# A linear-attention and softplus-FFN kernel: z turned in 32x32 blocks on VectorE and written as rows, and the first two FFN blocks taken through the weights together

## The chip, the cores and the metric

The kernel runs on one core of a Trainium2 chip. Five engines work side by side, each through its own queue in order: TensorE (PE, with its weight loads PEld), VectorE (DVE), ScalarE (ACT), GpSimd (POOL) and SyncE (SP). SyncE only issues DMAs here, and all DMAs of the kernel are issued by it. An instruction waits at the head of its queue until what it needs is there, and all that is queued behind it waits too. The metric is the device time of one execution in microseconds, the median over several runs.

## The reference

Attention with random features for 8 batches of 8 heads, 576 tokens, 64 dimensions and 128 features, then a feed-forward network with softplus over all 4608 tokens:

```python
q_p, k_p = phi(q * scale), phi(k * scale)     # exp(x @ omega.T - |x|^2/2 - max) / sqrt(m)
kv = np.einsum('bhsm,bhsd->bhmd', k_p, v)
z = np.sum(k_p, axis=2)
num = np.einsum('bhsm,bhmd->bhsd', q_p, kv)
den = np.einsum('bhsm,bhm->bhs', q_p, z)[..., None] + 1e-06
x = (num / den)                               # (4608, 512) after a transposition of heads
h = x @ w_in                                  # 512 -> 2048
g = np.maximum(h, 0.0) + np.log1p(np.exp(-np.abs(h)))
out = g @ w_out                               # 2048 -> 512
```

## The kernel before

Heads are handled in quads of four: 16 quads, two for each batch. For a quad, keys and queries come in five units of tokens (u = 0 to 4). A unit is loaded (L369 to L377 for batches 0 and 1, L489 and L494 later), squared and summed for its norms, split into a rounded part and a rest (L508, L512), projected on TensorE (L400 or L518), joined, reduced to its maximum, and exponentiated on ScalarE (L437 or L542). Keys are multiplied with v (L606, or L662 in batch 0); the last such product of a quad gives kv and, in an extra column, z.

What is done with z matters here. z of a quad lies as 128 partitions (features) by 4 (heads), and den needs it as rows of 128 features spread over all partitions. In batch 0 TensorE does this (`rows`, L686). In the 14 later quads it goes through DRAM: `z` (L616, VectorE) writes the tile, `out_z` (L624) stores it across, so that each element of 4 bytes is a piece by itself, and `in_z` (L628) reads the 4 x 128 numbers back as one row, broadcast to 128 partitions, as zb. `den` (L729, VectorE) multiplies the query features with zb and sums; `invert`, `divide` (L738, VectorE or GpSimd) and `blocks` (L761) follow; the turned features go through DRAM once more (L771, L774 out, L784 in), and `num` (L852) makes x, which is kept as a rounded part xh and a rest xl.

The FFN takes x in blocks: four of 256 tokens and seven of 512. For each of 16 slices fc of the hidden layer, `plan_step` lays 12 matmuls into h (L902 to L904), softplus on ScalarE and VectorE (L908 to L925), and 3 matmuls for every 128 tokens into acc (L931 to L933). The 32 weight slices are loaded at the start (L283) as 64-bit words and converted on ScalarE and VectorE (L291 to L310); wi and wo of a slice are needed by the first block that uses it.

No order is written by hand. Every step is a `Work` with the engines that can run it, costs, a due time and the buffers that it takes; `in_order` lays all of them out greedily by assumed costs, and due times say who goes first among those that can start. The numbers in the tables (LATE, PATIENCE, the offsets on each `due`) set the order and nothing else. `with_fill` puts matmuls without use (`fill`, L1043) where it expects TensorE to wait. For out_z the planner of before assumes `dma(1.3, 1.6, 0.3)`: 1.3 us until the transfer starts, 1.6 on the wires, 0.3 until it has landed.

The eight banks of PSUM are two for "at", two for "h" and four for "acc". Projections of batch 1 draw on "at" and "acc" (`room["more"]`).

Of the kernel before, what the change touches and what calls it, by code (L numbers as in the profile page):

```python
# [19 lines left out]
P = 128  # L20
# [13 lines left out]
AHEAD = 213.44  # L34
MARGIN = 0.00

LATE = {"num": 1.25, "turn": 5.44, "project": 0.85, "blocks": 0.00, "out": 0.27, "in": 2.55, "store": 0.24, "outer": 0.27}
START = {"SP": 0.75, "ACT": 1.9, "PE": 4.6}
SLOW = 7.59
FILL = 5.58  # L40
UNTIL = 93.76
HEAT = 2.95
EXTRA = 0.00
WINDOW = 3.4133
PATIENCE = {"PE": 0.00, "DVE": 0.01, "ACT": 0.00, "POOL": 1.23, "SP": 1.02}
LEAN = {"DVE": 0.81, "POOL": 0.50, "ACT": 0.00}
SPREAD = ((0, 24.76), (18.30, 71.16))
# [136 lines left out]
def favor_softplus_kernel(ctx, tc, q0, k0, qx, qy, kx, ky, vv, om, wi, wo, out):  # L184
# [16 lines left out]
    at.tile([P, 80], F32, name="gap")  # L201
# [72 lines left out]
    def plan_weights(nm, fc, due):  # L274
# [34 lines left out]
        def low_part(e):  # L309
# [5 lines left out]
            "SP", dma(0.65, 1.22, 1.7), due - 2.62, load, spare={} if last else {"w": 2},  # L315
# [5 lines left out]
        a = do(("ACT", "DVE"), (aw, dw2), due - 3.09, low_bits, after=[l], port=True)  # L321
        b = do("ACT", aw, due + 0.16, rebias, after=[l])
        c = do("DVE", dw, due - 3.03, joined, after=[a, b], port=True)
        d = do(
            ("ACT", "DVE"), (aw, dw), due + 0.20, high_part, after=[c] + (in_w if last else []), take=[("w", box, "w")], port=True,
# [3 lines left out]
        return do(("DVE", "POOL"), (dw, pw), due - 6.73, low_part, after=[d], give=[(box, "raw")], port=True)  # L329
# [14 lines left out]
    def plan_unit(q, kind, us, due, early):  # L344
# [83 lines left out]
        def exponent(j):  # L428
# [12 lines left out]
            "SP", read(size), due - 9.14, load, behind=prev.get("load"),  # L441
# [3 lines left out]
        if kind == "k" and not early:  # L445
            for i in range(len(us)):
                ldv.append(do(
                    "SP", dma(0.7, 1.0, 0.7), due + 28.88, lambda i=i: load_v(i), behind=ld, take=[("v", b, ("vs", i))]
                ))
        s = do(("POOL", "ACT"), (pool(w), act(w)), due + 7.71, squares, after=[ld])  # L450
        r, sm = None, [("sm", b, "sms")]
        if not cols:
            r = do("DVE", dve(w), due + 2.54, norms, after=[s], behind=prev.get("norms"), take=sm)
# [3 lines left out]
            "PE", 0.19 + (0.46 if cols else 0.23) * nt, due - 2.23, project, after=[ld] + ([s] if cols else []),  # L457
# [19 lines left out]
        for i in range(len(us)):  # L477
            plan_queries(q, us[i], due - 5.54 * i, b, es, f"{nm}_{i}", i, i == len(us) - 1)

    def plan_split(q, kind, u, due):  # L480
# [59 lines left out]
        def exponent(t):  # L540
# [4 lines left out]
            "SP", read(n * (P + D) * P * 4), due - 46.21, load, behind=prev.get("load"), take=[("x", b, "x")],  # L545
        )
        prev["load"], ldv = ld, []
        if kind == "k":
            ldv = [do("SP", dma(0.7, 1.0, 0.7), due + 5.80, load_v, behind=ld, take=[("v", b, ("vs", 0))])]
        s = do(("POOL", "ACT"), (pool(n * D), act(n * D)), due + 8.16, squares, after=[ld])  # L550
        h = do(("ACT", "DVE"), (act(n * P), dve(n * P, 2)), due - 4.34, rounded, after=[ld], take=[("ts", b, "ts")], port=True)
        h = do(("DVE", "POOL"), (dve(n * P) + 0.12, 1.12 * pool(n * P)), due - 0.80, rest, after=[h, parted], give=[], port=True)
        r = do(
            "DVE", dve(n * D), due + 20.76, norms, after=[s, h], behind=prev.get("norms"), take=[("sm", b, "sms")],
# [4 lines left out]
            "PE", 0.118 * n, due - 1.78, project, after=[h], behind=(prev.get("project"), q.zc if kind == "q" else None),  # L559
# [5 lines left out]
        for t in range(n // 2):  # L565
            a = do(
                "ACT", act(2 * M, PSUM), due + 0.31, lambda t=t: aside(t), after=[p], behind=a,
                take=[] if t else [("ph", b, ("phs", 0))], spare={"ph": 1}, soon={} if t or n < 4 else {p: 0.22},
            )
            es.append(do("DVE", dve(2 * M), due - 1.57, lambda t=t: join(t), after=[a], give=[(b, ("ppb", t))]))  # L570
        m = do("DVE", dve(n * M), due + 6.81, maxima, after=es + [r])
        m = do("DVE", 0.33, due - 0.16, bias, after=[m], port=True)
# [20 lines left out]
    def plan_sums(q, keys, due, deps):  # L593
# [20 lines left out]
        def z():  # L614
            q.z = at.tile([P, 16], F32, name=f"z{q.nm}", tag=q.slots["z"], bufs=1)[:, :4]
            nc.vector.scalar_tensor_tensor(q.z, y["kv"][:, :, D], rm, q.kvp[:, :, D], ALU.mult, ALU.add)  # L616

# [4 lines left out]
        def out_z():  # L622
            q.zd = dram.tile([4, P], F32, name=f"zd{q.nm}", tag="zd", bufs=2)
            nc.sync.dma_start(q.zd.rearrange("c m -> m c"), q.z)  # L624
# [9 lines left out]
        for k, (b, i, u) in enumerate(keys):  # L634
            m = do(
                "PE", 0.836 if u < 4 else 0.418, due + 0.62, lambda k=k: outer(k), after=[m] if k else [x for x, _ in deps],
# [4 lines left out]
        if first:  # L641
            q.part = do("ACT", 0.29, due - 25.64, part, after=[m] + ([quads[q.n - 1].kvl] if q.n > 2 else []), give=[(y, "bank")])
            return
        a = do("DVE", 0.1, due - 8.97, z, after=[m, q.part], take=[("z", q.slots, "z")])
        q.kvl = do("DVE", 0.35, due + 7.75, whole, after=[m, a] + old, give=[(y, "bank")])
        r = do("SP", dma(1.3, 1.6, 0.3), due - 18.33, out_z, after=[a], give=[(q.slots, "z")])
        q.zc = do("SP", dma(1.7, 1.6, 0.95), due + 34.19, in_z, after=[r], take=[("zb", q.slots, "zb")])

    def plan_early_keys(q, u, due, b, es):

        def outer():
# [15 lines left out]
            "PE", 0.836 if u < 4 else 0.418, due + 27.40, outer, after=es + [q.kvm], heat=1040,  # L667
# [6 lines left out]
        def z():  # L674
            q.z = at.tile([P, 16], F32, name=f"z{q.nm}", tag=q.slots["z"], bufs=1)[:, :4]
# [15 lines left out]
        def copy():  # L691
# [3 lines left out]
        a = do("DVE", 0.07, due + 29.06, z, after=[q.kvm], take=[("z", q.slots, "z")])  # L695
        q.kvl = do("ACT", 0.32, due + 4.48, high, after=[q.kvm, a], give=[(q.slots, "kv")])
        r = do(
            "PE", 0.86, due + 12.41, rows, after=[a], heat=2048, take=[("any", q.slots, "zp"), ("zb", q.slots, "zb")],
            give=[(q.slots, "z")],
        )  # L700
        q.zc = do("ACT", 0.48, due - 14.62, copy, after=[r], give=[(q.slots, "zp")])
# [10 lines left out]
    def plan_queries(q, u, due, bu, es, nm, first, last):  # L712
# [65 lines left out]
        def in_blocks(qt, o, sizes):  # L778
# [13 lines left out]
            "DVE", 0.87, due - 2.57, den, after=es + [q.zc], steps=4, soon={es[1]: 0.43} if q.b > 1 and u < 4 else {},  # L792
# [3 lines left out]
        d = do("DVE", 0.09, due + 0.43, invert, after=[d])  # L796
# [356 lines left out]
```

## Time and profile before

| | us |
|---|---|
| median of 3 runs | 1118.53 |
| lowest, highest | 1115.6, 1123.72 |
| profiled execution, its own time | 1131.58 |
| its span | 1129.8 |
| granted TensorE clock, mean | 0.962 |

The profile is of one execution. Busy times say how long an engine worked; a wait in a timeline stands in brackets ahead of the instruction that ended it, with the instruction that released it behind the arrow. The granted clock is 1 or 0.5 at any moment; a mean of 0.95 over a stretch says that a tenth of it ran at half. A matmul's duration contains its way through the array, so consecutive matmuls overlap: the distance of their starts is what one costs. For a DMA the table of issues gives the time from issue to landing.

### The profile page before, as it was taken

The page shows a single profiled execution, that of the slowest core. Times are in us where ns is not written, and L with a number is a line of the kernel's source. Part 1 is how long each engine was busy: PE and PEld are TensorE (multiplying, and loading weights), DVE is VectorE, ACT ScalarE, POOL GpSimd, SP SyncE. Part 2 cuts the span into 40 slices and gives each one's busy share as a digit, 9 for nine tenths or more (in the row PEclk, how much of TensorE's full clock was granted, in tenths as well). Part 3 has the DMA queues.
Part 4 walks back from the last instruction along what each step waited for, and adds up shares of the span by engine and source line. Part 5 has one row for each costly group of instructions (what it writes and reads, how often), then busy time and mean ns, then how long its engine had stood idle before and what let it go on. Part 6 is the DMA issues. An engine that isn't in the chain of part 4 may idle for free. (4 is left out here: it accounts for less than half of the span.)

```text
span 1129.8 us, 17905 instructions
## 1 busy us (share of the span) xinstructions
PE 1044.1 (92%) x5609; PEld 867.4 (77%) x5609; DVE 752.5 (67%) x2345; ACT 762.1 (67%) x1946; POOL 147.9 (13%) x173
## 2 busy tenths in 40 slices
PE   9689898998998989898979998979899799999998
PEld 6578786887886878687768786868778687888886
DVE  5899675776877867787867786868667733222222
ACT  6999666776867766777677786757665645444443
POOL 0021212122221211212110111102010100000000
PEclk9899898999998989899989999989989899999999
DMA  9941554534544446545454645563245402000001
GB/s 338 349 155 52 62 160 113 148 104 103 161 103 148 113 131 106 149 135 138 94 135 135 136 113 106 159 129 96 83 124 99 107 15 80 1 1 19 19 1 38
DMA packets 123278, 125.82 MB, mean 111 GB/s; under 512 B 23216, under 2 KB 98096, under 8 KB 123184
## 3 DMA queue, kind: packets, MB, share of 16 engines
q1 hardware_dynamic: 123184, 124.68, 41.5%
q8 instruction: 45, 0.74, 0.3%
q14 instruction: 49, 0.40, 0.1%
HBM read 98.66 MB, written 25.98 MB: 110 GB/s over the span
## 5 line engine op out<-in xcount | busy, mean ns | idle before, releaser
L902 PE MATMUL h<-xh,wi 128*128 128x512 f32 (+1 forms) x704 | 255.6, 363 | 4.6 <-DVE u L917 4.6
L903 PE MATMUL h<-xl,wi 128*128 128x512 f32 (+1 forms) x704 | 251.1, 357 | 0.0
L904 PE MATMUL h<-xh,wi 128*128 128x512 f32 (+1 forms) x704 | 250.1, 355 | 0.0
L931 PE MATMUL acc<-wo,gh 128*128 128x512 f32 x576 | 233.7, 406 | 0.0
L932 PE MATMUL acc<-wo,gh 128*128 128x512 f32 x576 | 229.9, 399 | 0.0
L933 PE MATMUL acc<-wo,gl 128*128 128x512 f32 x576 | 229.2, 398 | 0.0
L917 DVE SCALAR_TENSOR_TENSOR u<-h,u 128x512 f32<-128x512 f32 (+1 forms) x176 | 103.1, 588 | 160.2 <-ACT u L914 159.1
L908 ACT ACTIVATE u<-h 128x512 f32<-128x512 f32 (+1 forms) x176 | 91.2, 519 | 134.9 <-PE h L904 130.4
L902 PEld LDWEIGHTS h<-xh,wi 128*128 128x128 f32 x704 | 136.8, 194 | 28.9 <-DVE u L917 5.7
L903 PEld LDWEIGHTS h<-xl,wi 128*128 128x128 f32 x704 | 136.5, 194 | 18.4
L904 PEld LDWEIGHTS h<-xh,wi 128*128 128x128 f32 x704 | 135.9, 193 | 18.8
L921 ACT CAST gh<-u 128x512 fp32r<-128x512 f32 (+1 forms) x172 | 93.2, 542 | 58.4 <-PE acc L933 27.6
L933 PEld LDWEIGHTS acc<-wo,gl 128*128 128x128 f32 x576 | 110.9, 193 | 24.6
L931 PEld LDWEIGHTS acc<-wo,gh 128*128 128x128 f32 x576 | 110.9, 193 | 24.0 <-issue 4.5
L932 PEld LDWEIGHTS acc<-wo,gh 128*128 128x128 f32 x576 | 111.1, 193 | 17.8
L925 DVE TENSOR_TENSOR gl<-u,gh 128x512 fp32r<-128x512 f32 (+1 forms) x120 | 77.6, 647 | 52.4 <-ACT gh L921 51.5
L911 ACT ACTIVATE u<-u 128x512 f32<-128x512 f32 (+1 forms) x176 | 97.4, 555 | 3.1
L914 ACT ACTIVATE u<-u 128x512 f32<-128x512 f32 (+1 forms) x176 | 97.1, 554 | 2.5
L729 DVE CUSTOM_DVE_ANT_0 restq<-phq,zb 128x128 f32<-128x128 f32 x280 | 73.5, 294 | 18.9 <-DMA zb<-zd 11.2
L542 ACT ACTIVATE phk<-phk,smk 128x128 f32<-128x128 f32 x216 | 70.1, 392 | 11.7 <-DVE smk L538 11.6
L925 POOL TENSOR_TENSOR gl<-u,gh 128x256 fp32r<-128x256 f32 (+1 forms) x56 | 50.3, 900 | 182.2 <-ACT gh L921 158.0
L738 POOL TENSOR_TENSOR phq<-phq,dnq 128x512 f32<-128x512 f32 (+1 forms) x44 | 40.7, 925 | 254.0 <-DVE dnq L734 116.6
(122 smaller groups left out, 1522.4 us busy)
## 6 DMA issues: line engine op xcount, KB each, us to landing
xk<-ky SPq DMA_DIRECT2D x48, 384.0 KB, 3.8
xq<-qy SPq DMA_DIRECT2D x48, 384.0 KB, 3.6
qdq<-restq SPq DMA_DIRECT2D x56, 256.0 KB, 2.5
out<-o SPq DMA_DIRECT2D x36, 256.0 KB, 2.1
vk<-vv SPq DMA_DIRECT2D x70, 130.0 KB, 3.2
rawi<-wi SPq DMA_DIRECT2D x16, 512.0 KB, 6.6
rawo<-wo SPq DMA_DIRECT2D x16, 512.0 KB, 5.2
q<-qdq SPq DMA_DIRECT2D x64, 128.0 KB, 3.8
```

The lines of the kernel that those rows point to most:

```text
L902: nc.tensor.matmul(b["h"], wh, xh[:, cc, t], start=cc == 0, stop=False)
L903: nc.tensor.matmul(b["h"], wh, xl[:, cc, t], start=False, stop=False)
L904: nc.tensor.matmul(b["h"], wl, xh[:, cc, t], start=False, stop=cc == NCC - 1)
L908: nc.scalar.activation(b["u"], b["h"], AF.Abs)
L911: nc.scalar.activation(b["u"], b["u"], AF.Exp, scale=-1.0)
L914: nc.scalar.activation(b["u"], b["u"], AF.Ln, bias=1.0)
L917: nc.vector.scalar_tensor_tensor(b["u"], b["h"], 0.0, b["u"], ALU.max, ALU.add)
L921: (nc.scalar.copy if e == "ACT" else nc.vector.tensor_copy)(b["gh"], b["u"])
L925: (nc.vector if e == "DVE" else nc.gpsimd).tensor_tensor(b["gl"], b["u"], b["gh"].bitcast(F32), ALU.subtract)
L931: nc.tensor.matmul(acc[tt], gh, w2[fc][:, 0], start=fc == 0, stop=False)
L932: nc.tensor.matmul(acc[tt], gh, w2[fc][:, 1], start=False, stop=False)
L933: nc.tensor.matmul(acc[tt], gl, w2[fc][:, 0], start=False, stop=fc == NFC - 1)
```

## The change

Three things are done.

1. z. The tile for z becomes 128 x 32 (`z_wide`, two of them, filled with zeros once), of which four columns are used. `z_turn` on VectorE transposes it in blocks of 32 x 32, so that partitions 32i to 32i + 3 hold features 32i to 32i + 31 of the four heads as rows. `out_z` becomes four DMAs, one for each i, each of four rows of 32 numbers. `in_z` is as before.
2. The first two FFN blocks (256 tokens each) are planned as a pair: for each slice fc, the step of block 0 and the step of block 1 are planned together, block 1 due 7.32 us after block 0. Each block's order within itself is kept by its own `chain`.
3. The planner's numbers are new throughout, and so are the fillers: 8 of 512 columns at the start in place of 16 of 512 to 64.

```diff
-AHEAD = 213.44
+AHEAD = 295.87
...
+    z_wide = [at.tile([P, 32], F32, name=f"z{i}") for i in range(2)]
+    for t in z_wide:
+        nc.vector.memset(t, 0.0)
...
         def z():
-            q.z = at.tile([P, 16], F32, name=f"z{q.nm}", tag=q.slots["z"], bufs=1)[:, :4]
+            q.z = z_wide[int(q.slots["z"][-1])][:, :4]
             nc.vector.scalar_tensor_tensor(q.z, y["kv"][:, :, D], rm, q.kvp[:, :, D], ALU.mult, ALU.add)
+
+        def z_turn():
+            q.zr = at.tile([P, 32], F32, name=f"zr{q.nm}", tag="zr", bufs=1)
+            nc.vector.transpose(q.zr, z_wide[int(q.slots["z"][-1])])
...
             q.zd = dram.tile([4, P], F32, name=f"zd{q.nm}", tag="zd", bufs=2)
-            nc.sync.dma_start(q.zd.rearrange("c m -> m c"), q.z)
+            for i in range(4):
+                r = slice(i * 32, (i + 1) * 32)
+                nc.sync.dma_start(q.zd[:, r], q.zr[i * 32 : i * 32 + 4])
...
-        r = do("SP", dma(1.3, 1.6, 0.3), due - 18.33, out_z, after=[a], give=[(q.slots, "z")])
-        q.zc = do("SP", dma(1.7, 1.6, 0.95), due + 34.19, in_z, after=[r], take=[("zb", q.slots, "zb")])
+        a = do("DVE", 0.11, due + 9.09, z_turn, after=[a], port=True)
+        r = do("SP", dma(2.0, 0.4, 1.4, 4), due + 19.39, out_z, after=[a], give=[(q.slots, "z")])
+        q.zc = do("SP", dma(1.7, 1.6, 0.95), due + 49.11, in_z, after=[r], take=[("zb", q.slots, "zb")])
...
-        for fc in range(NFC):
-            plan_step(i, t0, n, fc, FIRST + 2.00 * k, acc, box)
-            k += max(1, n / 384)
+        if i < PAIR:
+            pair.append((i, t0, n, [], box, {}))
+        else:
+            pair = [(i, t0, n, [], box, box)]
+        if i >= PAIR - 1:
+            for fc in range(NFC):
+                for x, (b, o, w, acc, _, chain) in enumerate(pair):
+                    plan_step(b, o, w, fc, FIRST + (PACE * fc + GAP * x if len(pair) > 1 else 2.00 * k), acc, box, chain)
+                    k += max(1, n / 384)
+            box.update(chain)
```

SyncE's queue at the sixth of the 14 z, before (zd is z in DRAM, zb its copy on all partitions, xq, xk and vk are loads, qdq the turned query features):

```order
L624 DMA zd_1_5005<-z_1_4997 128x4x1
L628 DMA zb_1_5039<-zd_1_5005 128x512
L489 DMA xq_1_1_5053<-qy 128x768
L774 DMA qdq_0_0_4569<-restq_0_4_5000 64x4x64 x2
L489 DMA xk_0_2_5107<-ky 128x768
```

And after the change:

```order
L634 DMA zd_1_5046<-zr_1_5037 4x32 x4
L493 DMA xq_1_1_5098<-qy 128x768
L638 DMA zb_1_5108<-zd_1_5046 128x512
L785 DMA qdq_0_0_4610<-restq_0_4_5057 64x4x64 x2
L493 DMA xk_0_2_5158<-ky 128x768
```

One DMA has become four, and the load of xq has moved ahead of the read back, which waits for them.

VectorE at the same z, before (the rows that read zb_0 are den of the quad before):

```order
L538 SCALAR_TENSOR_TENSOR smk_0_0_4953<-smk_0_0_4953 128x4
L616 SCALAR_TENSOR_TENSOR z_1_4997<-kv_1_2_False,kvp_1_4754 128x4
L729 ISA restq_0_4_5000,dnq_0_4_4999<-phq_0_4_4916,zb_0_4368 64x128
L729 ISA dnq_0_4_4999 64x1
L729 ISA restq_0_4_5000,dnq_0_4_4999<-phq_0_4_4916,zb_0_4368 64x128
```

And after the change:

```order
L620 SCALAR_TENSOR_TENSOR z_94<-kv_1_2_False,kvp_1_4767 128x4
L541 SCALAR_TENSOR_TENSOR smq_0_4_4946<-smq_0_4_4946 128x2
L542 SCALAR_TENSOR_TENSOR smq_0_4_4946<-smq_0_4_4946 128x2
L628 SCALAR_TENSOR_TENSOR kvs_1_5033<-kv_1_2_False,kvp_1_4767 128x256
L624 STREAM_TRANSPOSE zr_1_5037<-z_94 128x32
L928 SCALAR_TENSOR_TENSOR u_8_5006<-h_8_4967,u_8_5006 128x512
```

The transposition stands four rows behind z here (two to eight over the 14), and the first den that reads this quad's own zb stands 34 rows behind z where it stood 29; on the mean of the 14 it is 37 rows against 31.

TensorE where the second FFN block begins, before (h_15 is the last slice of block 0, the new h_0 is block 1; wi_185 is the weight slice that block 0 began with):

```order
L902 MATMUL h_15_1660<-xh,wi_1645 128x256
L903 MATMUL h_15_1660<-xl,wi_1645 128x256
L904 MATMUL h_15_1660<-xh,wi_1645 128x256
L902 MATMUL h_0_1683<-xh,wi_185 128x256
L903 MATMUL h_0_1683<-xl,wi_185 128x256
L904 MATMUL h_0_1683<-xh,wi_185 128x256
```

And after the change (acc_0_916 and acc_1_925 are block 0's sums, wo_800 its third slice):

```order
L942 MATMUL acc_1_925<-wo_800,gh_2_991 128x512
L943 MATMUL acc_1_925<-wo_800,gh_2_991 128x512
L944 MATMUL acc_1_925<-wo_800,gl_2_1052 128x512
L858 MATMUL xp_1_256_0_1091<-qq_1_2_0_1054,kvs_1_659 64x320 x2
L858 MATMUL xp_1_256_1_1094<-qq_1_2_0_1054,kvs_1_659 64x320 x2
L913 MATMUL h_0_1103<-xh,wi_273 128x256
L914 MATMUL h_0_1103<-xl,wi_273 128x256
```

Block 1 now begins behind the third slice of block 0, as soon as its x is there (xp_1_256), and not behind the last one.

More of the change, by code (lines that the diff above doesn't have):

```diff
@@ L328, in plan_weights @@
             in_w.append(d)
[L329 removed]
+        return do(("DVE", "POOL"), (dw, pw), due - 5.66, low_part, after=[d], give=[(box, "raw")], port=True)
     class Quad:
@@ L440, in plan_unit @@
         ld = do(
-            "SP", read(size), due - 9.14, load, behind=prev.get("load"),
+            "SP", read(size), due + 4.42, load, behind=prev.get("load"),
             take=[("w" if early else "x", b, "x")], spare={"w": 2} if early else {},
@@ L544, in plan_split @@
         ld = do(
-            "SP", read(n * (P + D) * P * 4), due - 46.21, load, behind=prev.get("load"), take=[("x", b, "x")],
+            "SP", read(n * (P + D) * P * 4), due - 12.21, load, behind=prev.get("load"), take=[("x", b, "x")],
         )
@@ L548, in plan_split @@
         if kind == "k":
[L549 to L552, printed above, removed]
+            ldv = [do("SP", dma(0.7, 1.0, 0.7), due + 19.97, load_v, behind=ld, take=[("v", b, ("vs", 0))])]
+        s = do(("POOL", "ACT"), (pool(n * D), act(n * D)), due + 32.96, squares, after=[ld])
+        h = do(("ACT", "DVE"), (act(n * P), dve(n * P, 2)), due + 0.43, rounded, after=[ld], take=[("ts", b, "ts")], port=True)
+        h = do(("DVE", "POOL"), (dve(n * P) + 0.12, 1.12 * pool(n * P)), due - 1.92, rest, after=[h, parted], give=[], port=True)
         r = do(
-            "DVE", dve(n * D), due + 20.76, norms, after=[s, h], behind=prev.get("norms"), take=[("sm", b, "sms")],
+            "DVE", dve(n * D), due + 6.15, norms, after=[s, h], behind=prev.get("norms"), take=[("sm", b, "sms")],
             give=[(b, "x")],
@@ L791, in plan_queries @@
         d = do(
-            "DVE", 0.87, due - 2.57, den, after=es + [q.zc], steps=4, soon={es[1]: 0.43} if q.b > 1 and u < 4 else {},
+            "DVE", 0.87, due - 33.48, den, after=es + [q.zc], steps=4, soon={es[1]: 0.43} if q.b > 1 and u < 4 else {},
             take=[("dn", b, "dns")] + ([("ph", bu, ("rest", first))] if q.b else []),
@@ L823, in plan_queries @@
         h = do(
-            ("ACT", "DVE"), (act(n * M, PSUM), dve(n * M)), due + 19.16, turned, after=[t], give=[(b, "tpb")],
+            ("ACT", "DVE"), (act(n * M, PSUM), dve(n * M)), due + 4.59, turned, after=[t], give=[(b, "tpb")],
         )
@@ L970, in store @@
                 nc.sync.dma_start(out[t0 + tt * P : t0 + (tt + 1) * P, :], o["t"])
-            a = do("DVE", 0.34, due - 9.45, left, after=[ends[tt]], take=[("t2", o, "s")])
-            r = do("ACT", 0.27, due - 18.81, right, after=[a], give=[(box, ("acc", i, tt))])
-            do("SP", dma(0.25, 0.8, 1.05), due - 20.96, store, after=[a, r], give=[(o, "s")], late=LATE["store"])
+            a = do("DVE", 0.34, due + 14.47, left, after=[ends[tt]], take=[("t2", o, "s")])
+            r = do("ACT", 0.27, due - 24.01, right, after=[a], give=[(box, ("acc", i, tt))])
+            do("SP", dma(0.25, 0.8, 1.05), due - 29.57, store, after=[a, r], give=[(o, "s")], late=LATE["store"])
     assert NQ == 2
```

144 lines of the change are left out of this document (72 added, 72 removed).

## The prediction, made blind

> **What bounds the kernel now.** I read the page's busy times first, then windows of the span, then the waits of SyncE's queue and the table of transfers, then the timeline round one place, and last who waits for TensorE's late inputs.
>
> ```profile
> span 1129.8 us, 17905 instructions
> PE 1044.1 (92%) x5609; PEld 867.4 (77%) x5609; DVE 752.5 (67%) x2345; ACT 762.1 (67%) x1946; POOL 147.9 (13%) x173
> ```
>
> TensorE is busy 92% of the span. The windows (columns: length, busy us and count of PE, PEld, DVE, ACT, POOL, granted clock, DMA share, GB/s) say where the rest lies. The first four are stages; the next two are two of the 14 stretches that each begin when z is sent to DRAM and end when TensorE is at full clock again; the last line sums all 14.
>
> ```profile
> 0.00:57.50 57.50, 45.43 (x307) 35.05 (x307) 41.27 (x188) 45.92 (x123) 4.44 (x12) 0.94 0.90 338
> 57.50:116.00 58.50, 55.93 (x399) 48.14 (x400) 55.00 (x167) 55.97 (x147) 11.73 (x14) 0.98 0.30 100
> 116.00:890.00 774.00, 708.53 (x3854) 592.26 (x3853) 580.83 (x1847) 548.17 (x1482) 127.02 (x143) 0.95 0.50 123
> 890.00:1124.20 234.20, 234.18 (x1054) 191.92 (x1052) 74.57 (x145) 111.35 (x195) 4.68 (x5) 1.00 0.06 19
> ...
> 325.50:350.50 25.00, 19.44 (x92) 15.46 (x92) 16.07 (x51) 15.12 (x41) 3.02 (x4) 0.86 0.49 109
> ...
> 622.00:642.00 20.00, 18.41 (x88) 15.21 (x87) 14.20 (x46) 12.75 (x32) 3.25 (x4) 1.00 0.73 128
> ...
> sum 318.00, PE 254.13 PEld 206.80 DVE 202.50 ACT 186.78 POOL 47.10; mean PE 18.15 PEld 14.77 DVE 14.46 ACT 13.34 POOL 3.36
> ```
>
> From 890 us on, when attention is over, TensorE is never idle. From 116 to 890 us it is idle 774 - 708.5 = 65.5 us, and 318 - 254.1 = 63.9 us of that lies in the 14 stretches after a z. Outside them it is busy 454.4 of 456 us. So nearly all idle time of the long stage belongs to one event, 14 times over. The waits of the SyncE queue, the table of transfers and the timeline name it:
>
> ```profile
> SPq L628 <- DMA zd<-z: 93.0, 13, 9.8
> ...
> xk<-ky SPq DMA_DIRECT2D x48, 384.0 KB, 3.8
> qdq<-restq SPq DMA_DIRECT2D x56, 256.0 KB, 2.5
> out<-o SPq DMA_DIRECT2D x36, 256.0 KB, 2.1
> zb<-zd SPq DMA_DIRECT2D x14, 256.0 KB, 5.2
> qdq<-restq SPq DMA_DIRECT2D x28, 64.0 KB, 4.0
> zd<-z SPq DMA_DIRECT2D x14, 2.0 KB, 9.9
> ```
> ```profile
> 325.52 0.38 SPq L624 DMA_DIRECT2D zd<-z  x1
> 325.95 0.50 SPq L771 DMA_DIRECT2D qdq<-restq  x1
> 329.25 0.35 SPq L489 DMA_DIRECT2D xk<-ky  x1
> 329.69 2.75 SPq L494 DMA_DIRECT2D vk<-vv  x1
> 336.71 0.33 SPq L628 DMA_DIRECT2D zb<-zd  x1
> ...
> 339.74 0.42 ACT L498 ACTIVATE xk<-xk 128x256 f32<-128x256 f32 x1 [6.55 <-DMA xk<-ky]
> ...
> 339.15 0.39 PE L904 MATMUL h<-xh,wi 128*128 128x512 f32 x1
> 344.69 1.31 PE L518 MATMUL ppk<-oms,tk 128*128 128x256 f32 x4 [5.15 <-DVE tk L512]
> 345.80 0.63 PE L931 MATMUL acc<-wo,gh 128*128 128x512 f32 x1
> 346.23 0.63 PE L932 MATMUL acc<-wo,gh 128*128 128x512 f32 x1
> ...
> 350.47 0.40 PE L904 MATMUL h<-xh,wi 128*128 128x512 f32 x1
> 350.70 0.39 PE L902 MATMUL h<-xh,wi 128*128 128x512 f32 x1
> ```
>
> The smallest transfer of the program, 2 KB, takes the longest to land: 9.9 us against 2.1 for the 256 KB output store. It is written across the grain, 4 bytes at a time. The read back (L628) waits for it, and every load behind L628 waits too: 93 us in 13 waits. A load issued between the two is also late: xk, issued at 329.25, is used at 339.74, 10.5 us on, where such a load lands in 3.8. Then ACT and DVE stand, and TensorE 5.15 us behind them. After that its matmuls follow each other in 0.43 us instead of 0.23: half clock until 350.47.
>
> **The change, part by part.** *Loss in the 14 trips.* Idle: 63.9 us. Clock: 774 x (1 - 0.95) = 38.7 us are withheld in the stage. Where the engine was idle this cost nothing: in the stretch shown, 25 x 0.14 x 2 = 7.0 us at half clock, of which matmuls ran 344.69 to 350.47 = 5.8 us, or 0.8. So 0.8 x 38.7 = 31 us. Together 95 us, 6.8 a trip.
>
> *Removed and added.* The one DMA becomes four, each of four rows of 128 bytes, and a VectorE transposition comes ahead.
>
> ```profile
> L624 SPq DMA_DIRECT2D zd<-z x14: 377/378/426, 116.0 to 864.2; - x14
> L616 DVE SCALAR_TENSOR_TENSOR z<-kv_False,kvp x14: 122/160/165, 115.8 to 864.0; 128x4 f32<-128x4 f32 x14
> L761 DVE STREAM_TRANSPOSE restq<-phq 128x256 f32<-128x256 f32 x14 | 6.2, 442 | 2.7 <-POOL phq L738 2.2
> DVE restq L729 <- DMA zb<-zd: 11.2, 3, 3.9
> PE ppk L518 <- POOL tk L512: 7.0, 1, 7.0
> PE ppq L518 <- DVE phq L527: 6.0, 1, 6.0
> ```
>
> SyncE issues three more, 3 x 0.38 = 1.1 us a trip, 16 us in all, on a queue that mostly waits. For the landing no row shows 16 packets of 128 bytes. Bounds: 2.1 us (the output store, also SBUF to DRAM) and 4.0 (the 64 KB piece of qdq, the only other write in rows below 512 bytes). I take 3.0. The hold from first issue to read back falls from 9.9 to 1.1 + 3.0 = 4.1 us (3.2 to 5.1), 5.8 us less (4.8 to 6.7). The wait of TensorE averages 63.9 / 14 = 4.6 us and reaches 7.0, so what the hold loses covers nearly every wait. The transposition is 32 columns wide: above the 0.16 us of L616 on four, below 0.44 us on 256; 14 x 0.2 = 3 us on VectorE, between other work. Two fills of 32 columns come once at the start, also below 0.44 us each. The read back itself still takes 5.2 us; behind it stands the first den (L729) on VectorE, which waited 11.2 us in 3 of 14 trips. The new order puts it further from z, as the fences of the section on the change show for SyncE and VectorE.
>
> The Trainium skill, in DMA: Bandwidth & Descriptors, section Specifications, asks for at least 512 B a transfer, below which the engine reads, modifies and writes. That speaks against rows of 128 B. By the rows, 256-byte pieces land in 4.0 us against 2.5 for 512-byte ones; so by the rule the hold would be 5.1 us, not 4.1, and the time at most 14 x 1 = 14 us higher.
>
> *The table of numbers* lays every queue anew. On TensorE the 14 trips come at much the same places: 162 FFN matmuls of 3840 stand ahead of the first z now, 228 before, and 2799 ahead of the last, 2757 before. I cost the rest of it at nothing, since the cover (FFN matmuls between attention steps) is the same; if it is gone at a place, TensorE's next projection is late there, as in the rivals.
>
> *What then limits.* With all 95 us gone the stage would take 679 us and VectorE, 580.8 + 3 = 584 us, would be 86% busy. Outside the trips it is (580.8 - 202.5) / 456 = 83% busy today while TensorE hardly waits. If 83% is all that the hand-overs allow, the stage takes 584 / 0.83 = 703 us. From 57.5 to 116 us it was 94% busy and TensorE still 55.9 of 58.5, so more may be had. I take the middle, 691: 83 us won, of 71 to 95.
>
> *Two blocks through the weights together.* Same matmuls, same conversions; each pair of prepared weights now has two blocks' work waiting.
>
> ```profile
> 57.51 0.90 PE L745 MATMUL tpq<-ident,xq 128*128 128x128 f32 x3 [9.04 <-ACT xq L437]
> 133.99 0.69 DVE L310 TENSOR_TENSOR wo<-rawo,wo 128x512 fp32r<-128x512 f32 x1 [0.44 <-ACT wo L307]
> ```
>
> The last weights are ready at 135 us, so the first block lasts until then; but TensorE loses only 2.6 us between 57.5 and 116, where ACT (55.97 of 58.5) and VectorE (55.0) are the full engines, and they get no less to do. Before 57.5 us it loses 57.5 - 45.4 = 12.1 us, 9.04 of it behind ACT's exponents, which stand behind weight conversions; the new order has such a row of conversions again, covered in part by 15 filler matmuls. I take 3 us won, between 5 lost (half the largest wait once more) and 12 won.
>
> *Sum.* 1131.58 us of the profiled execution (span and 1.8 round it) - 83 - 3 = 1045. It stands 13 us, 1.2%, above the median of the runs, 1118.53. If everything scales, 1045 x 0.9885 = 1033; if the 13 us all sit in the trips, the median loses 82 there, wins 83/95 of it, 72, and 1118.5 - 72 - 3 = 1044. I forecast 1038.
>
> **Rivals.** *The wait moves to the read back and to VectorE* (chance 0.15). For it: zb still takes 5.2 us, and VectorE is in order. Against it: den waited in 3 of 14 trips only, and now stands later. The shortest wait after a trip that still halved the clock was 2.73 us; one of 1.59 left it at 1.00 (the stretch from 622 above):
>
> ```profile
> 238.30 1.20 PE L518 MATMUL ppq<-oms,tq 128*128 128x256 f32 x4 [2.73 <-DVE phk L527]
> 640.67 0.81 PE L518 MATMUL ppq<-oms,tq 128*128 128x256 f32 x4 [1.59 <-DVE phk L527]
> 222.80:241.30 18.50, 15.77 (x99) 14.18 (x98) 10.66 (x34) 11.76 (x37) 4.21 (x5) 0.91 0.32 80
> ```
>
> If 2.7 us stay in each trip, with 18.5 x 0.09 = 1.7 us of clock, 14 x 4.4 = 62 of the 95 us stay: 1131.6 - 33 = 1099, x 0.9885 = 1086. The Trainium skill, TensorE: Matmul & The Clock Gate, section What's actually happening, halves the clock only after an idle window of about 3.4 us; by that the 2.7 us waits would cost no clock and this rival would come to 1062. The row disagrees: 2.73 us was enough.
>
> *The four writes land one after another* (0.07), so that the change doesn't do what it says: 4 x 2.1 + 1.1 = 9.5 us, the hold as long as now. For it: nothing here shows rows of one 512-byte line written by four DMAs. Against it: the jam behind 512 packets would still be gone. About 1115, within 1%.
>
> *Pairing starves the second batch* (0.05), the other side. Two open blocks hold all four acc banks of PSUM until the last weights, and projections of batch 1 draw on the same banks. It decides once it delays the blocks after the pair by over 86 us plus 11, 97 in all, that is if TensorE stood for most of the time from 57.5 to 182 us; then 1131 or more. Against it: in the order of matmuls, as many FFN matmuls (414) stand ahead of batch 1's last kv matmul as before.
>
> **How the numbers follow.** The forecast, with its own range of 1013 to 1060, has 0.73. Its low end: 95 + 12 us won, 1025 x 0.9885 = 1013; its high end: 71 won, 5 lost, the 13 us inside the trips. With the first rival, the range is 1013 to 1087; outside it lie the other two rivals. A measurement can tell about 1% from no change. Faster by over 1%: 0.73 + 0.15 = 0.88, less 0.01 for a mix of small losses: 0.87. Within 1%: 0.08. Slower: 0.05.
>
> **What would show it.** Right: zd lands in 2 to 4 us; the wait of L638 (the read back's new line) for it falls from 93 us to below 40; TensorE's idle time in the 14 stretches falls below 20 us; clock in the long stage 0.98 or more; VectorE 84 to 86% busy there; the time to 116 us within 5 us of now. Wrong: zd at 8 us or more (the writes queue up); idle time at the same places but released by zb or den (first rival); a stretch between 60 and 180 us in which projections wait for PSUM (third).

## The result, and the profile after

| | us |
|---|---|
| before, median of 4 runs on the same chip (lowest, highest) | 1121.12 (1115.6, 1127.48) |
| after, median of 4 runs (lowest, highest) | 1028.63 (1027.98, 1032.76) |
| after / before, with its 95% interval | 0.9181 [0.9123, 0.9239] |
| after, profiled execution: its own time, its span | 1032.76, 1031.0 |

The change won 92.5 us. Among the experiments below, one execution of one_by_one_again and one of a_jam, the profiled one, took some 23 us longer than the others of their kernel; the ratios leave both out, and the extra time of a_jam's lies ahead of its first z. The page of the changed kernel begins like this:

```profile
span 1031.0 us, 17929 instructions
PE 1011.7 (98%) x5606; PEld 844.2 (82%) x5606; DVE 757.9 (74%) x2359; ACT 761.3 (74%) x1944; POOL 155.0 (15%) x177
```

TensorE is busy 98% of the span where it was 92%, with 5606 matmuls in place of 5609. The windows of the changed kernel, in the columns of the prediction (length, busy us and count of PE, PEld, DVE, ACT and POOL, granted clock, DMA share, GB/s), are the four stages, with the end of attention at 800 us in place of 890, then one of the 14 stretches that follow a z, and the sum of all 14:

```profile
0.00:57.50 57.50, 50.26 (x358) 38.40 (x359) 44.92 (x210) 47.81 (x125) 6.95 (x16) 0.96 0.92 347
57.50:116.00 58.50, 55.84 (x402) 48.08 (x403) 54.35 (x159) 56.82 (x157) 16.02 (x17) 0.98 0.38 118
116.00:800.00 684.00, 680.56 (x3839) 573.11 (x3836) 583.40 (x1839) 546.89 (x1470) 130.07 (x142) 1.00 0.48 136
800.00:1027.00 227.00, 225.04 (x1014) 184.56 (x1012) 75.07 (x156) 109.38 (x194) 1.97 (x2) 1.00 0.08 25
...
294.40:320.00 25.60, 25.36 (x132) 20.21 (x131) 22.52 (x63) 19.42 (x52) 4.02 (x5) 1.00 0.53 156
...
sum 310.50, PE 310.12 PEld 256.57 DVE 269.37 ACT 247.86 POOL 54.22; mean PE 22.15 PEld 18.33 DVE 19.24 ACT 17.70 POOL 3.87
```

In the 14 stretches TensorE is now idle for 310.50 - 310.12 = 0.4 us, where it was 63.9, and the long stage runs at a clock of 1.00 instead of 0.95. VectorE is busy 583.4 of its 684 us there, 85%, and TensorE still idle only 3.4 us. The waits of SyncE's queue, and SyncE's timeline at the z that begins the stretch shown, are the counterparts of the rows of before with 93.0 us in 13 waits and a read back 11.2 us behind its store:

```profile
SPq L638 <- DMA zd<-zr: 9.6, 6, 2.5
```
```profile
294.41 1.29 SPq L634 DMA_DIRECT2D zd<-zr  x4
295.81 0.39 SPq L782 DMA_DIRECT2D qdq<-restq  x1
297.10 0.36 SPq L493 DMA_DIRECT2D xk<-ky  x1
297.56 0.41 SPq L498 DMA_DIRECT2D vk<-vv  x1
298.15 0.33 SPq L638 DMA_DIRECT2D zb<-zd  x1
```

The read back is issued 3.7 us after the first of the four stores, and three other transfers fit between. Over the 14 z this hold averages 3.6 us (2.3 to 5.3), against 10.4 (8.3 to 12.7) before, each taken from such a timeline as the start of the read back less the start of the first store. The shortest one has nothing but one gap in it:

```profile
98.05 1.32 SPq L634 DMA_DIRECT2D zd<-zr  x4
100.37 0.36 SPq L638 DMA_DIRECT2D zb<-zd  x1
```

In the full table of groups the transposition stands with 14 x 0.2 us (busy, mean ns, idle before):

```profile
L624 DVE STREAM_TRANSPOSE zr<-z 128x32 f32<-128x32 f32 x14 | 2.8, 201 | 0.0
```

### The profile page after: what moved, and what is told of

The parts are those of the page before. It is cut to its first block, busy times and chain, and to the rows that moved or that the text cites. A ratio compares the mean times of both kernels' runs of the same rounds, so it can differ in the third digit from the quotient of the medians.

```text
span 1031.0 us, 17929 instructions
## 1 busy us (share of the span) xinstructions
PE 1011.7 (98%) x5606; PEld 844.2 (82%) x5606; DVE 757.9 (74%) x2359; ACT 761.3 (74%) x1944; POOL 155.0 (15%) x177
## 4 chain that ended last, share of the span: by engine, by line
PE 90%; ACT 3%; DVE 3%; DMA 2%; issue 1%; SPq 0%; DVEq 0%; ACTq 0%
PE acc L942 13%; PE h L913 12%; PE acc L943 12%; PE acc L944 12%; PE h L914 12%; PE h L915 12%; PE kv_True L610 4%; PE xp L863 3%; PE ppq L522 2%; PE ppk L522 2%; PE kv_False L610 2%; PE ppq L404 1%; PE ppk L404 1%; PE kv L673 1%; DMA xk<-k 1%; DMA xq<-qy 1%
## 5 line engine op out<-in xcount | busy, mean ns | idle before, releaser
L913 PE MATMUL h<-xh,wi 128*128 128x512 f32 (+1 forms) x704 | 250.8, 356 | 1.5 <-DVE u L928 1.4
L914 PE MATMUL h<-xl,wi 128*128 128x512 f32 (+1 forms) x704 | 247.8, 352 | 0.0
L915 PE MATMUL h<-xh,wi 128*128 128x512 f32 (+1 forms) x704 | 247.6, 352 | 0.0
L942 PE MATMUL acc<-wo,gh 128*128 128x512 f32 x576 | 230.3, 400 | 0.7 <-ACT o L978 0.7
L943 PE MATMUL acc<-wo,gh 128*128 128x512 f32 x576 | 225.7, 392 | 0.0
L944 PE MATMUL acc<-wo,gl 128*128 128x512 f32 x576 | 225.0, 391 | 0.0
L913 PEld LDWEIGHTS h<-xh,wi 128*128 128x128 f32 x704 | 133.4, 190 | 24.4 <-issue 3.0
L915 PEld LDWEIGHTS h<-xh,wi 128*128 128x128 f32 x704 | 133.5, 190 | 18.1
L914 PEld LDWEIGHTS h<-xl,wi 128*128 128x128 f32 x704 | 133.7, 190 | 17.5
L932 ACT CAST gh<-u 128x512 fp32r<-128x512 f32 (+1 forms) x174 | 94.5, 543 | 63.9 <-PE acc L944 26.8
L942 PEld LDWEIGHTS acc<-wo,gh 128*128 128x128 f32 x576 | 108.6, 189 | 24.9 <-issue 4.9
L943 PEld LDWEIGHTS acc<-wo,gh 128*128 128x128 f32 x576 | 108.8, 189 | 17.0
L749 POOL TENSOR_TENSOR phq<-phq,dnq 128x512 f32<-128x512 f32 (+1 forms) x49 | 45.7, 934 | 290.6 <-DVE dnq L745 118.1
L936 POOL TENSOR_TENSOR gl<-u,gh 128x256 fp32r<-128x256 f32 (+1 forms) x61 | 57.1, 937 | 184.2 <-ACT gh L932 167.1
L740 DVE CUSTOM_DVE_ANT_0 restq<-phq,zb 128x128 f32<-128x128 f32 x280 | 78.1, 318 | 8.5 <-ACT phq L441 4.2
L546 ACT ACTIVATE phk<-phk,smk 128x128 f32<-128x128 f32 x216 | 70.2, 394 | 10.7 <-DVE smk L542 10.6
```

The lines of the kernel that those rows point to most:

```text
L913: nc.tensor.matmul(b["h"], wh, xh[:, cc, t], start=cc == 0, stop=False)
L914: nc.tensor.matmul(b["h"], wh, xl[:, cc, t], start=False, stop=False)
L915: nc.tensor.matmul(b["h"], wl, xh[:, cc, t], start=False, stop=cc == NCC - 1)
L932: (nc.scalar.copy if e == "ACT" else nc.vector.tensor_copy)(b["gh"], b["u"])
L936: (nc.vector if e == "DVE" else nc.gpsimd).tensor_tensor(b["gl"], b["u"], b["gh"].bitcast(F32), ALU.subtract)
L942: nc.tensor.matmul(acc[tt], gh, w2[fc][:, 0], start=fc == 0, stop=False)
```

## The experiments

Three questions were open. How much of the 92.5 us comes from z, and how much from the pair and the new numbers? Is it the hold of SyncE, the small pieces themselves, or both? And what about the pieces costs time? The first four kernels ran on one chip, where before took 1137.55 us (1132.36 to 1142.07); the next four on another, with before at 1116.89; the last four there too, with before at 1113.75. All ratios are against before on the same chip and in the same group.

### The parts apart

The changed kernel with its numbers and its pair, but z stored across again by one DMA (a_across; the transposition still runs, but nobody reads it):

```diff
-            for i in range(4):
-                r = slice(i * 32, (i + 1) * 32)
-                nc.sync.dma_start(q.zd[:, r], q.zr[i * 32 : i * 32 + 4])
+            nc.sync.dma_start(q.zd.rearrange("c m -> m c"), q.z)
```

> The changed kernel in its own order, with z stored across again by one DMA in pieces of 4 bytes; the transposition still runs, and nobody reads its result. If the 14 trips of z made the gain, nearly all of it goes: 1105 to 1140 us, zd lands in 8 to 11 us again, and TensorE is idle 50 us or more in the stage from 116 us on, with half clock after many waits. If the new order or the pairing made it, the time stays below 1050 us.

It took 1112.92 us, ratio 0.9785 [0.9757, 0.9814]. Its window over the long stage, and the wait of SyncE's queue:

```profile
116.00:890.00 774.00, 720.83 (x3921) 603.37 (x3921) 599.19 (x1893) 561.19 (x1507) 130.86 (x144) 0.96 0.50 122
```
```profile
SPq L636 <- DMA zd<-z: 100.9, 14, 10.0
```

The old picture is back nearly whole with that one DMA: SyncE stands 100.9 us in 14 waits, TensorE is idle 774 - 720.8 = 53.2 us in the same 774, the clock is 0.96. So the new order and the pair don't hide the trips. They are worth 1137.55 - 1112.92 = 24.6 us with the store across in place, more than they turn out to be worth with rows (below). Part of that is probably a trip that costs less in the new order: the idle time of this window is 53.2 us here against 65.5 in the profile of before, which is of another set of runs.

The kernel of before, its order and numbers, with z turned and written as rows, and no pair (b_rows; an unused tile shrinks by the 64 columns that the two z_wide take):

```diff
+    z_wide = [at.tile([P, 32], F32, name=f"z{i}") for i in range(2)]
...
+            q.zr = at.tile([P, 32], F32, name=f"zr{q.nm}", tag="zr", bufs=1)
+            nc.vector.transpose(q.zr, z_wide[int(q.slots["z"][-1])])
...
-            nc.sync.dma_start(q.zd.rearrange("c m -> m c"), q.z)
+            for i in range(4):
+                r = slice(i * 32, (i + 1) * 32)
+                nc.sync.dma_start(q.zd[:, r], q.zr[i * 32 : i * 32 + 4])
```

> The kernel before in its own order and with its own numbers, with z turned on VectorE and stored by four DMAs as rows; the blocks are not paired. If the trips made the gain: 1035 to 1060 us, with less than 20 us of idle TensorE in the stage with the trips. If the new order is needed for it: above 1080 us.

It took 1035.77 us, ratio 0.9108 [0.9081, 0.9136]. The long stage, in the same window:

```profile
116.00:890.00 774.00, 772.12 (x4299) 648.60 (x4298) 622.66 (x1949) 594.51 (x1572) 132.17 (x148) 1.00 0.45 127
```

TensorE is idle 1.9 us of 774, in the old order. The window reaches past the end of attention here; up to 800 us, too, it is idle 1.9 us. The rows do nearly all of it by themselves, 101.8 us on this chip.

The pair alone in the kernel of before, with the two numbers that place its blocks (b_pair), and the changed kernel with its blocks one by one (a_one_by_one):

```diff
-        for fc in range(NFC):
-            plan_step(i, t0, n, fc, FIRST + 2.00 * k, acc, box)
-            k += max(1, n / 384)
+        if i < PAIR:
+            pair.append((i, t0, n, [], box, {}))
...
```
```diff
-    PAIR = 2
+    PAIR = 1
```

> The kernel before with the first two blocks paired and nothing else changed; z is stored across. If the trips are what costs: 1105 to 1130 us, no difference that can be measured. If pairing made the gain: below 1080 us. If pairing starves the second batch: above 1135 us.

> The changed kernel with the first two FFN blocks one after the other, all numbers kept. If pairing is worth what the prediction put on it (3 us, between 5 lost and 12 won): 1024 to 1041 us. If pairing made a large part of the gain: above 1060 us.

The pair alone took 1144.29 us, ratio 1.005 [1.0019, 1.0081]: slightly slower. (The 1135 us of its expectation is no mark here, since before itself takes 1137.55 on this chip.) Its windows of the early stages, 20 us of the first of them, the longest wait in these 20 us, and SyncE's wait:

```profile
57.50:116.00 58.50, 52.38 (x322) 44.07 (x321) 48.14 (x144) 49.79 (x127) 14.78 (x15) 0.81 0.33 109
116.00:205.00 89.00, 81.89 (x572) 70.86 (x570) 62.29 (x217) 63.73 (x190) 19.14 (x23) 0.98 0.36 99
...
80.00:100.00 20.00, 15.70 (x90) 12.60 (x89) 17.71 (x36) 18.07 (x47) 5.82 (x6) 0.83 0.20 63
```
```profile
90.15 0.58 PE L902 MATMUL h<-xh,wi 128*128 128x256 f32 x1 [3.94 <-DVE u L917]
```
```profile
SPq L628 <- DMA zd<-z: 116.6, 14, 11.0
```

From 57.5 to 116 us TensorE loses 6.1 us instead of 2.6, and the clock is 0.81 instead of 0.98. Not all of that is the pair's: rows alone, without a pair, show a clock of 0.87 there in one of their two profiles (rows_again, below). The pair's own part lies from 80 to 100 us, where TensorE loses 4.3 us, 3.94 of it in one wait behind VectorE, at a clock of 0.83, and before loses 0.3 at 1.00; the rows with the pair (b_rows_pair, below) have the same wait, 3.93 us. So in the old numbers the pair costs something early, and the trips still hold SyncE 14 times. The changed kernel without its pair took 1043.28 us, ratio 0.9167 [0.9139, 0.9195], some 14 us above what the whole change takes and just above the range expected for a pair worth 3 us. Beside b_rows on the same chip the new numbers alone are 7.5 us slower, and the intervals don't overlap.

### What in the store across costs time

On the second chip the changed kernel itself was run again (after_again), with a long hold put back without the small pieces (a_hold: three copies from DRAM to DRAM stand between the row stores and the read back, each waiting for the one before), and with the small pieces put back without the hold (a_jam: behind the read back, z is also stored across into a tile that nobody reads):

```diff
+            for h in range(3):
+                zn = dram.tile([4, P], F32, name=f"ze{q.nm}_{h}", tag=f"ze{h}", bufs=2)
+                nc.sync.dma_start(zn, q.zd)
+                q.zd = zn
```
```diff
+            ze = dram.tile([4, P], F32, name=f"ze{q.nm}", tag="ze", bufs=2)
+            nc.sync.dma_start(ze.rearrange("c m -> m c"), z_wide[q.n % 2][:, :4])
```

> The changed kernel itself, for comparison on this chip: 1025 to 1036 us.

> The changed kernel with three copies more from DRAM to DRAM, each waiting for the last, between the store of z as rows and the read back; no small pieces. They hold SyncE's queue, and put off the read back, for some 6 to 7 us more, about as long as before the change, but leave the DMA engines free. If the loss of the 14 trips came from the queue held and the read back late: 1090 to 1125 us. If it came from the 512 small pieces in the way of other transfers: below 1045 us.

> The changed kernel with one more store of z, across in pieces of 4 bytes, to a place that nobody reads, issued behind the read back. Nothing waits for it as data; it only stands in the way of later transfers. If the small pieces in the way were the cost: 1070 to 1125 us. If the queue held at the read back was the cost: below 1045 us.

| | us | ratio |
|---|---|---|
| after_again | 1030.04 | 0.9236 [0.9198, 0.9274] |
| a_hold | 1086.71 | 0.9744 [0.9704, 0.9783] |
| a_jam | 1075.80 | 0.965 [0.9602, 0.9698] |

SyncE's timeline in a_hold at a z, and its long stage up to 790 us:

```profile
312.49 1.29 SPq L634 DMA_DIRECT2D zd<-zr  x4
314.66 0.53 SPq L637 DMA_DIRECT2D ze<-zd  x1
316.52 2.30 SPq L637 DMA_DIRECT2D ze<-ze  x2
...
320.54 0.42 SPq L642 DMA_DIRECT2D zb<-ze  x1
```
```profile
116.00:790.00 674.00, 641.86 (x3542) 537.27 (x3541) 538.48 (x1693) 505.50 (x1363) 122.56 (x136) 0.97 0.44 126
```

The read back comes 8.05 us after the first store here, 8.7 us on the mean of the 14 (7.8 to 10.0), 5.1 us more than in the changed kernel. The time rose by 1086.71 - 1030.04 = 56.7 us, 4.05 us for each z, and TensorE is idle again, 32 us of 674, with the clock at 0.97. So a long hold is costly with no piece of 4 bytes in it. It came out shorter than expected, 5.1 us in place of 6 to 7, and the time just below the expected 1090 us. The copies also add 14 x 96 packets, which are no likely cost: a kernel below adds 14 x 528 and loses nothing.

The jam is costly with no hold in front of the read back: 1075.80 - 1030.04 = 45.8 us. If only the one or only the other cost time, one of the two kernels would have stayed near 1030. In a_jam it is the loads that come late: the waits of ScalarE for xk and xq (total, times, longest), in a_jam and then, for xk, in the kernel a_jam_apart below, which loses nothing:

```profile
ACT xk L502 <- DMA xk<-ky: 27.9, 12, 4.7
ACT xq L502 <- DMA xq<-qy: 24.9, 12, 6.0
```
```profile
ACT xk L502 <- DMA xk<-ky: 7.1, 12, 1.4
```

For xq a_jam_apart waits 3.5 us. In the kernel of before both costs lie in the same ten microseconds, which may be why they don't add up: 57 + 46 = 103 us, against some 75 to 82 that the rows won. No kernel with both put back was run on this chip.

What the jam is made of, one further kernel tells (a_jam_apart). It stores the same 512 pieces of 4 bytes, but each 512 bytes from the next:

```diff
-            ze = dram.tile([4, P], F32, name=f"ze{q.nm}", tag="ze", bufs=2)
-            nc.sync.dma_start(ze.rearrange("c m -> m c"), z_wide[q.n % 2][:, :4])
+            ze = dram.tile([4, P, P], F32, name=f"ze{q.nm}", tag="ze", bufs=2)
+            nc.sync.dma_start(ze[:, :, 0].rearrange("c m -> m c"), z_wide[q.n % 2][:, :4])
```

> As the run with one more store of z across behind the read back (1075.8 us, 46 above the changed kernel), but each of the 512 pieces of 4 bytes goes to a line of 512 bytes of its own. If each small piece costs by itself, the time is as there: 1065 to 1085 us. If the pieces hold each other up because 128 of them go into one line of 512 bytes: below 1045 us.

It took 1028.78 us, ratio 0.9237 [0.9196, 0.9277], and the changed kernel beside it (after_third) 1028.79, ratio 0.9235 [0.9205, 0.9266].

> The changed kernel itself, for comparison on this chip: 1025 to 1036 us.

The pages count the same packets for a_jam and for a_jam_apart:

```profile
DMA packets 123727, 125.86 MB, mean 115 GB/s; under 512 B 23664, under 2 KB 98544, under 8 KB 123632
```
```profile
DMA packets 123727, 125.86 MB, mean 123 GB/s; under 512 B 23664, under 2 KB 98544, under 8 KB 123632
```

14 x 512 more small pieces than the changed kernel has cost nothing when they lie 512 bytes apart, and 45.8 us when 128 of them share 512 bytes. So it is not the number of pieces or their size alone, but where they land. From the first z to the last a_jam takes 847.59 - 120.08 = 727.5 us and a_jam_apart 781.27 - 97.99 = 683.3, so the loss lies where the stores are. That neighbouring pieces are written one behind another, with other transfers behind them, is an inference from this pair of runs: no view shows the memory itself, and distances between 4 and 512 bytes were not tried.

### What the pair and the numbers are worth

Two kernels of the first group were run again beside after_third: rows alone (rows_again) and the changed kernel without its pair (one_by_one_again). On the second chip rows and pair in the old numbers had also run (b_rows_pair).

> The kernel before with its own numbers, z as rows and the first two blocks paired. Beside z as rows alone (1035.8 us on another chip) this is what pairing is worth in the old numbers: within 5 us of it by the prediction, since VectorE and ScalarE are full there either way. Below 1028 us pairing wins something by itself; above 1045 us it loses without numbers of its own.

> The kernel before with z as rows alone, beside the changed kernel on the same chip. What is left between the two is what pairing and the new numbers are worth together: 3 us by the prediction, with -5 and 12 as its bounds.

> The changed kernel with the first two blocks one after the other, beside the changed kernel on the same chip. 1043.3 us before on another chip. If pairing is worth 3 us: within 5 us of the changed kernel. If the new numbers were made for the pair: 10 us or more slower than it.

| | pair | numbers | us | ratio |
|---|---|---|---|---|
| rows_again | no | old | 1039.29 | 0.9328 [0.9298, 0.9358] |
| b_rows_pair | yes | old | 1047.55 | 0.9388 [0.9338, 0.9437] |
| one_by_one_again | no | new | 1042.83 | 0.9361 [0.933, 0.9393] |
| after_third | yes | new | 1028.79 | 0.9235 [0.9205, 0.9266] |

The new numbers alone come out 3.5 us above rows alone, and the pair alone 0.006 in the ratio. The intervals of these ratios overlap, since before itself varies by 10 us, but the times of the kernels themselves hardly do: rows_again took 1035.16 to 1040.52 us in six runs, one_by_one_again 1041.17 to 1043.67 in five, and b_rows_pair 1042.02 to 1050.41 in four. With the 7.5 us of the first chip, either alone loses some us. Both together win 1039.29 - 1028.79 = 10.5 us. The windows up to 205 us show where. Below each kernel's windows stands the sum of the fillers in the same windows (busy us of PE and PEld alone, so these rows have fewer columns). First after_third:

```profile
0.00:57.50 57.50, 52.17 (x363) 40.29 (x364) 45.29 (x210) 47.88 (x125) 6.90 (x16) 0.94 0.92 347
57.50:116.00 58.50, 54.83 (x407) 46.96 (x406) 54.98 (x165) 57.05 (x159) 16.43 (x17) 1.00 0.37 118
116.00:205.00 89.00, 88.56 (x618) 76.99 (x619) 71.88 (x241) 73.31 (x217) 23.82 (x29) 1.00 0.46 133
...
sum 205.00, PE 14.89 PEld 9.21; mean PE 4.96 PEld 3.07
```

Then rows_again, and the wait of 9 us that it has kept from before:

```profile
0.00:57.50 57.50, 45.46 (x310) 35.38 (x311) 41.73 (x193) 46.56 (x126) 4.44 (x12) 0.92 0.89 338
57.50:116.00 58.50, 56.35 (x362) 48.28 (x362) 50.62 (x154) 51.41 (x136) 10.65 (x13) 0.87 0.30 100
116.00:205.00 89.00, 88.69 (x644) 77.10 (x645) 73.08 (x260) 70.89 (x213) 22.70 (x28) 1.00 0.48 139
...
sum 205.00, PE 17.35 PEld 10.31; mean PE 5.78 PEld 3.44
```
```profile
56.82 1.97 PE L753 MATMUL tpq<-ident,xq 128*128 128x128 f32 x8 [9.00 <-ACT xq L441]
```

And one_by_one_again, with two rows of its fillers ahead of their sum:

```profile
0.00:57.50 57.50, 49.91 (x370) 38.63 (x370) 46.02 (x212) 48.59 (x127) 6.99 (x16) 1.00 0.92 347
57.50:116.00 58.50, 55.33 (x409) 46.74 (x408) 54.49 (x172) 58.23 (x158) 7.43 (x9) 1.00 0.39 127
116.00:205.00 89.00, 86.97 (x583) 74.39 (x583) 66.67 (x231) 66.91 (x202) 18.43 (x22) 1.00 0.42 121
sum 205.00, PE 192.21 PEld 159.76 DVE 167.18 ACT 173.73 POOL 32.85; mean PE 64.07 PEld 53.25 DVE 55.73 ACT 57.91 POOL 10.95
...
57.50:116.00 58.50, 5.11 (x18) 3.16 (x18) 1.00 0.39 127
116.00:205.00 89.00, 2.05 (x7) 1.24 (x7) 1.00 0.42 121
sum 205.00, PE 21.88 PEld 13.37; mean PE 7.29 PEld 4.46
```

A filler counts as busy but does no work, so it has to be taken off. TensorE's useful time to 205 us is then 195.56 - 14.89 = 180.7 us in after_third, 190.50 - 17.35 = 173.2 in rows_again, and 192.21 - 21.88 = 170.3 in one_by_one_again. The differences, 7.5 and 10.3 us, are not yet the loss, because a matmul at half clock is busy twice as long for the same work, and the clocks differ: rows_again is busy for 56.35 us of its second window at a clock of 0.87. The work itself can be counted from the traces as the columns of all matmuls started, fillers left out, at 0.23 us for 512 columns at full clock. By that count rows_again stands 3.9 us behind after_third at 57.5 us, 8.9 at 116 and 9.9 at 205, which is nearly the whole of its 10.5. One_by_one_again stands 0.8 ahead at 57.5 us, 3.2 behind at 116, 6.2 at 205 and 10.6 at 300, of the 14.0 by which it is slower.

Rows alone lose theirs in the wait of 9 us behind ScalarE and at the half clock behind it. In b_rows, the same kernel on the first chip, the wait is there too, but the clock of the second window is 0.98, and the count is 5.6 us behind at 205. So some 4 of the 10.5 us are half clock that not every run of rows alone has. The new numbers take the wait away, but with one block open there is not enough ready behind 57.5 us: 7.2 us go to fillers and 2.0 more to idle time behind 116 us. From 205 to 300 us another 1.8 us are idle; the rest of its loss was not followed up. With two blocks open TensorE has neither fillers nor more than 0.4 us of idle time from 116 to 205 us. No kernel went below the changed one by more than the runs can tell, so there is no better version among them.

## Why the prediction was right, and where it was off

*The bound* was right, and right in its mechanism. With the trips gone, the idle time of the long stage and its lost clock went with them; b_rows shows it for the store alone, and a_across shows the reverse. Of the 92.5 us, 10.5 belong to the pair and the numbers (from the second chip), which leaves 82 for z; the step had 83. The whole change won 85.0 and 86.9 us in the two sets on the second chip. By the chip the rows alone won from 74.5 us (1113.75 - 1039.29) to 101.8, so that the agreement to 1 us is partly luck; the size is right.

*Why the trip costs* was only half told. The prediction put the loss down to the hold of SyncE and named the jam only in passing, in a rival that kept the time near 1115 us although the jam would be gone: that puts the jam at next to nothing, and a_jam shows 45.8 us. a_hold and a_jam show two costs, each large enough alone. The sum came out right since one edit removes both.

*The hold* was taken to fall from 9.9 to 4.1 us, by 4.8 to 6.7. It fell from 10.4 to 3.6 on the mean, by 6.8, just beyond that end, because the stores land sooner than the 3.0 us assumed: the four issues take 1.3 us, and 2.3 us after the first of them the read back may go. The wait of the read back, 9.6 us in 6 cases, is far below the 40 us that was to show it right. The Trainium skill, DMA: Bandwidth & Descriptors, section Specifications, asks for 512 B or more for full rate, which spoke against rows of 128 B; the hold of 5.1 us that the prediction worked out for it from its rows isn't seen, with 3.6 on the mean. What the section says of a read, a modification and a write below that size fits the jam of pieces that lie side by side, though pieces as small that lie apart cost nothing measurable.

*The limit behind it* was mis-sized on the safe side. VectorE at 83% was taken as a possible bound, and 691 us for the stage as the middle. VectorE went to 85% over the stage and 87% in the trips (269.37 of 310.50), and TensorE is idle 3.4 us of 684. The 83% of before was what the work needed outside the trips, not what hand-overs allow.

*The transposition* took 0.20 us, as assumed, and TensorE waited for it once, 0.4 us.

*The pair, 3 us won of -5 to +12*, measured 10.5 together with the numbers. This is the term that was mis-sized. The step priced what was idle, 2.6 us from 57.5 to 116, and did not ask how much of the 9 us wait ahead of it the new order could fill with work (it goes nearly whole), nor what half clock follows that wait, nor that fillers count as busy. *The table of numbers, costed at nothing*, fails in the same place: it decides what the pair is worth, which loses a little in the old numbers (b_pair 1.005, b_rows_pair slower than rows_again) and wins 14.0 us in the new.

*The rivals.* The wait did not move to the read back: no wait of VectorE for zb is left, though it had 11.2 us before. The read back now comes early enough that den finds it there, and not because den stands further from z: in b_rows, with den at its old place, no such wait is left either. The four writes did not land one after another; 2.3 us rules that out. Pairing did not starve the second batch, but the doubt was sound in its direction: in the old numbers it costs, b_pair by 0.5% and not by the 97 us that the rival needed.

*The checks* that were listed held: idle time in the trips 0.4 us (below 20), clock 1.00 (0.98 or more), VectorE 85% (84 to 86). The time to 116 us is not directly comparable since the order differs; TensorE's busy time there rose from 101.4 to 106.1 us, and the first z comes at 98.05 instead of 116.03. The landing of zd has no time of its own in the table after, so only the read back bounds it.

*The level*: 1038 was 9.4 us above what was measured, 0.9%. The pair's 3 in place of 10.5 is 7.5 of them; the rest, 1.9 us, is less than the 2.6 us by which before itself differed between the two sets of runs. That the forecast lies in the middle between two ways of scaling, 1033 and 1044, makes part of this closeness luck. The high end of its range comes to 1062 by its own terms, not 1060, which changes nothing here.

## What to carry to other kernels

Where a tiny transfer takes longer to land than a large one, look at where its pieces land: 4-byte pieces side by side in memory cost here nearly as much by holding other transfers up as by the wait for them, and a 32x32 transposition of 0.2 us ahead of the store removes both. Price a hold on an in-order queue as hold times count, against the waits behind it, and then check that what would come next is a real limit: an engine's busy share between waits shows what the work needs, not what it can do. Take fillers and half clock into account before reading how full an engine is, and judge two edits that feed each other, like an open pair and the order around it, together and apart.

## What the runs showed of the hardware that was not expected

*Small pieces.* 512 pieces of 4 bytes cost 45.8 us over 14 stores when they lie side by side in 2 KB, and nothing that the runs can tell when they lie 512 bytes apart.

*Chips.* The kernel of before took 1113.75 to 1137.55 us in the four comparisons, by chip and group, while kernels that store rows lie much closer: rows alone 1035.77 and 1039.29, one by one 1043.28 and 1042.83 on the two chips. So what the store across costs seems to differ by chip, and with it the gain: the ratio of rows alone was 0.9108 on one and 0.9328 on the other. There was one group on the one chip and two on the other, so the chip as the cause is not shown.

*The clock.* In before a wait of 2.73 us halved the clock and one of 1.59 did not, which was read as a bound on the wait. TensorE's timeline and windows of the changed kernel show half clock behind a wait of 1.01 us:

```profile
757.20 3.14 PE L610 MATMUL kv_True<-vk,phk 128*128 128x65 f32 x24 [1.01 <-DVE xl L874]
```
```profile
756.00:759.70 3.70, 2.69 (x23) 2.50 (x23) 2.42 (x5) 3.67 (x11) 0.00 (x0) 1.00 0.63 121
759.70:763.10 3.40, 3.40 (x17) 2.44 (x17) 1.13 (x3) 1.71 (x6) 0.00 (x0) 0.50 0.70 250
```

Behind the wait come 24 products of only 65 columns, and then 3.4 us at half clock, in which TensorE is busy throughout. The length of the wait alone doesn't decide it, and one kernel in two runs shows that too. b_rows and rows_again are the same program; in the first a wait of 1.80 us leaves the clock at 1.00, in the second the same wait, 1.76 us, is followed by 3.4 us at half clock:

```profile
68.23 0.63 PE L753 MATMUL tpq<-ident,xq 128*128 128x128 f32 x4 [1.80 <-ACT xq L441]
68.20:72.20 4.00, 3.97 (x33) 3.74 (x35) 3.97 (x17) 3.73 (x10) 1.23 (x2) 1.00 0.87 289
```
```profile
71.64 0.63 PE L753 MATMUL tpq<-ident,xq 128*128 128x128 f32 x4 [1.76 <-ACT xq L441]
72.20:75.60 3.40, 3.40 (x18) 3.40 (x17) 3.37 (x17) 2.13 (x7) 0.86 (x1) 0.51 0.67 211
...
56.80:68.90 12.10, 12.08 (x63) 9.93 (x63) 7.83 (x46) 7.00 (x16) 0.00 (x0) 0.50 0.27 102
```

The last row is what follows the wait of 9 us in rows_again: 12 us at half clock with TensorE busy all the while, where b_rows is back at full clock some 3 us behind the same wait. So busy time alone doesn't bring the clock back either. The Trainium skill, TensorE: Matmul & The Clock Gate, section What's actually happening, has the clock halved after an idle window of about 3.4 us and full again after a busy one of that length; the 3.4 us of two of these stretches agree, but no idle time of that length stands ahead of either, and the stretch of 12 us is longer. From 60.0 to 67.3 us of it run products whose weights are 64 wide or that have two columns. That narrow products count as little work would fit both, but it is a guess that no run tested, and what decides stays open.
